# The start of a two-stage mixer kernel: the order of its first loads, and filling products on TensorE

## The chip, the cores and the metric

One core of a Trainium2 chip runs the whole program; the other cores of the chip are idle. The metric is the device time of one execution in microseconds (us), taken as the median of the runs shown.

## The reference, cut to what matters

Eight batches go through three stages: softmax attention inside chunks of 64 tokens, a mixer with a gate (moe), and a low-rank mixer with a wide channel layer (moe2).

```
attn = softmax(q_c @ k_c^T / 8); x = attn @ v_c           # 8 heads, 9 chunks of 64 tokens
h = relu(x @ w_in); u, v = halves of h (512 each)
v_n = (v - mean) / sqrt(var + 1e-6)                       # over the 512 channels
x = (u * (w_spatial @ v_n + b_spatial)) @ w_out
u = x + (x^T @ U @ V)^T;  out = u + relu(u @ w_ch1) @ w_ch2
```

## The kernel before, in words

Every large product is made of three half-precision products (`mm3`, lines 148 to 151): each operand is held as a high part and a low part, and high by high, high by low and low by high are summed. So an operand passes through ScalarE, which makes the high part, and through VectorE or GpSimd, which subtracts it from the original.

The weights arrive as 64-bit floats. To decode one tile of them, `dec_abs` (ScalarE, line 172) scales the upper words, `dec_bits` (VectorE, lines 179, 180 and 183) puts bits and sign back, and `dec_parts` makes the high part (ScalarE, line 190) and the low part (GpSimd, line 191). Eight such tiles, w_71 to w_78, are needed first: four for the half v of the first mixer (numbers 4 to 7, the tiles w_75 to w_78) and four for the half u (numbers 0 to 3, w_71 to w_74). `first_loads` (lines 423 to 459) loads them into rooms that are used later by other tiles, between the loads of the first five attention tiles; `gen_dec(0)` decodes them.

An attention tile holds two chunks of eight heads. The first nine tiles take a path of their own in single precision, `gen_first` (lines 494 to 530). For each: q is spread into a block-diagonal buffer (line 469, ScalarE, for tiles 0 to 4; by two DMAs, line 473, for 5 to 8); eight products give the scores (line 501); `a_softmax` takes maximum and difference on VectorE (384, 387) and the exponential on ScalarE (388); `a_norm` sums and divides on VectorE (393 to 396); four transpositions (514) and a copy on ScalarE (515) turn the result; eight products with v (522) give the output tile, whose high part ScalarE makes (409, or 416 for the fifth) and whose low part VectorE makes (410, 417). The values v are loaded into the tile's own `pt` space and copied on ScalarE into a block-diagonal buffer (line 484). All these buffers lie inside `wch`, the room of the later weights; tiles 5 to 8 use the places of tiles 2, 3, 4 and 2 again.

Then the first batch's mixer, `gen_moe(0)`, follows: five products with the v half of the weights (`pb<-w,xT` and `pb<-w,xd`), each evicted by ScalarE (637), normalised by VectorE and GpSimd (640 to 644, 649, 597 to 600) and scaled by VectorE (line 603, `ln_out`); eight groups with the u half (`pb<-xT,w`, evicted at line 663); the spatial product (`pb<-sp_m,vn`, with the tail of the last 64 tokens, `tl` and `vt`, in lines 679 and 680); the output product (`pb<-gt,w`); DMA transposes of it (`tr`, line 756), each one followed by a product with U (715 to 717) and V (731). The fifth `ln_out` feeds the tail: ScalarE copies it (614, 615), GpSimd makes the low part (616) and two DMAs move it (619).

The framework's scheduler decides the order of the instructions on each queue from the program's text and its priorities, so an edit in the text can move work that it doesn't name. The queue of SP issues nearly all loads, in order. Sixteen products of zeros (`NWARM`, line 450) stand at the start of TensorE's queue.

Of the kernel before, what the change touches and what calls it, by code (L numbers as in the profile page):

```python
# [8 lines left out]
F32 = mybir.dt.float32  # L9
F16 = mybir.dt.float16  # L10
# [21 lines left out]
PACE_B = 0.8  # L32
PACES = (0.0, 0.0, 1.0, 1.0, 1.0, 1.0, 0.9, 0.9)
NWARM = 16
SP_AFTER = 5
LDV = (3, 4)
MEMSET = (0, 1, 0, 1, 1)
# [63 lines left out]
def moe_kernel(  # L101
# [153 lines left out]
    def gen_dec(part):  # L255
# [17 lines left out]
        def run(names, loaded=False, step=1700.0):  # L273
            n = len(names)
            for i in range(-1, n + 2):
                if i + 1 < n and not loaded:
                    ld(names[i + 1])
                if 0 <= i < n:
                    dec_abs(names[i])
                if 0 <= i - 1 < n:  # L280
                    dec_bits(names[i - 1])
                    fin(names[i - 1])
                yield "wait", step
# [136 lines left out]

    wf = wch.rearrange("p f a k n -> p (f a k n)").bitcast(F32)

    def first_loads():

        room = []
# [22 lines left out]
        wp = ps_h.tile([128, 512], F32, tag="h", name="wp")  # L448
        for i in range(NWARM):
            nc.tensor.matmul(out=wp, lhsT=warm[:, 0:128], rhs=warm, start=True, stop=True)  # L450
        for i in range(5):
            first_qk(i)
            if i < 2:
                w()
            first_v(i)
            if i < 2:
                w()
        for i in range(4):
            w()

    def first_qk(i):
        qb, vb, kf, pt = first_bufs(i)
        if i < 5:
            qs = wf[:, 15360 + (i % 2) * 512:15360 + (i % 2 + 1) * 512]
            nc.sync.dma_start(out=qs, in_=q[i])
            nc.sync.dma_start(out=kf, in_=k[i])
            for c in range(2):
                r = slice(c * 64, (c + 1) * 64)
                nc.scalar.copy(out=qb[r, :, c, :], in_=qs[r].rearrange("p (h n) -> p h n", h=H))
            return  # L470
        for c in range(2):
            r = slice(c * 64, (c + 1) * 64)
# [2 lines left out]

    def first_v(i):
        qb, vb, kf, pt = first_bufs(i)
        vs = pt.rearrange("p a n -> p (a n)")
        if i in LDV:
            vs = sb.tile([128, 512], F32, tag="ldv", name="vs", bufs=1)  # L480
# [13 lines left out]
    def gen_first(lo, hi):  # L494

        for i in range(lo, hi):
            qb, vb, kf, pt = first_bufs(i)
            yield "wait", 2000.0
            sp = ps_acc.tile([128, H, 64], F32, tag=f"acc{i % 4}", name="sp")
            for h in range(H):  # L500
                nc.tensor.matmul(
                    out=sp[:, h, :], lhsT=qb[:, h].rearrange("p c n -> p (c n)"), rhs=kf[:, h * 64:(h + 1) * 64],
# [1 line left out]
                )  # L504
            se = kf.rearrange("p (h j) -> p h j", h=H)
            a_softmax(sp, se)
            yield "pe", 1000.0
            yield "wait", 2500.0
            a_norm(se, float(2 ** -10))
# [474 lines left out]
```

## Time and profile before

| | us |
|---|---|
| median of 3 runs (lowest, highest) | 1317.17 (1316.94, 1319.39) |
| the profiled execution, its own time | 1316.08 |
| its span, first to last instruction | 1314.3 |
| TensorE busy in the span | 1266.0 (96%) |
| VectorE, ScalarE, GpSimd busy | 529.8, 517.2, 517.3 |
| mean granted clock of TensorE, as a share of 2.4 GHz | 0.983 |

The profile is of one execution. 1.8 us of its time lie outside the span. Busy time is the time in which an engine ran at least one instruction that counts; the idle time before an instruction is put down to what ended it. PE is TensorE, PEld its weight loads, DVE VectorE, ACT ScalarE, POOL GpSimd, SP the queue that issues loads. A line number is that of the kernel's file.

### The profile page before, as it was taken

Reading aid. Unit: us, or ns where it says so; the run is one execution under the profiler, and the core shown is the slowest. Engines: PE = TensorE matmul, PEld = TensorE weight load, DVE = VectorE, ACT = ScalarE, POOL = GpSimd, SP = SyncE. Lnnn points to the kernel's source line nnn. Section 1 sums busy time; section 2 is a strip of 40 time slices with the busy share of each in tenths; the row PEclk is TensorE's granted clock in tenths of the full one; section 3 lists DMA queues with packets and bytes.
Section 4 is the critical chain, followed back from the end, with each engine's and each line's share of the span. In section 5 each row is a group of like instructions: output and inputs, shape, how many; then the busy total and the mean of one; then the engine's idle time right before and its main releaser. Section 6 shows DMA issues by size and latency. Waiting matters only on the chain.

```text
span 1314.3 us, 20540 instructions
## 1 busy us (share of the span) xinstructions
PE 1266.0 (96%) x8308; PEld 728.1 (55%) x8308; DVE 529.8 (40%) x945; ACT 517.2 (39%) x1061; POOL 517.3 (39%) x644
## 2 busy tenths in 40 slices
PE   7988888899999999999999999999999999999998
PEld 6676455445666556654665456645655565544443
DVE  8774797665343533334134514242113211221211
ACT  7765565545545433433344424323122212121110
POOL 6754887655555443534155415213111311020000
PEclk6899999899999999999999999999999999999999
DMA  8644253532223311321024101110011001000000
GB/s 285 198 143 117 88 168 100 124 103 82 61 65 77 89 33 39 77 51 42 4 65 93 49 1 33 36 41 5 0 24 34 13 0 26 20 24 1 32 0 32
DMA packets 99015, 81.43 MB, mean 62 GB/s; under 512 B 73828, under 2 KB 74468, under 8 KB 98920
## 3 DMA queue, kind: packets, MB, share of 16 engines
q1 hardware_dynamic: 97768, 75.92, 21.1%
q10 hardware_dynamic: 1152, 4.19, 0.9%
q8 instruction: 65, 1.06, 0.3%
q14 instruction: 30, 0.25, 0.1%
HBM read 53.62 MB, written 9.44 MB: 48 GB/s over the span
## 4 chain that ended last, share of the span: by engine, by line
PE 75%; DVE 8%; DMA 5%; ACT 4%; POOL 4%; issue 3%; SPq 0%; DVEq 0%; ACTq 0%; POOLq 0%
PE acc L149 8%; PE acc L151 8%; PE acc L150 8%; PE phid L151 8%; PE phid L150 8%; PE phid L149 8%; PE pb L149 7%; PE pb L150 7%; PE pb L151 7%; DVE dt L183 2%; DMA st<-in_wk_dram 2%; DVE dt L180 2%; DMA pt<-ph 1%; DMA vf<-in_v_dram 1%; DVE dt L179 1%
## 5 line engine op out<-in xcount | busy, mean ns | idle before, releaser
L815 DVE SCALAR_TENSOR_TENSOR hid<-phid,hid 128x512 f16<-128x512 f32 x144 | 99.1, 688 | 379.7 <-ACT hid L813 379.4
L150 PE MATMUL acc<-hid,wch 128*128 128x512 f16 x576 | 219.0, 380 | 0.4 <-DVE hid L815 0.4
L151 PE MATMUL acc<-hid,wch 128*128 128x512 f16 x576 | 219.1, 380 | 0.0
L149 PE MATMUL phid<-uT,wch 128*128 128x512 f16 x576 | 219.0, 380 | 0.0
L150 PE MATMUL phid<-uT,wch 128*128 128x512 f16 x576 | 218.9, 380 | 0.0
L151 PE MATMUL phid<-uT,wch 128*128 128x512 f16 x576 | 218.9, 380 | 0.0
L149 PE MATMUL acc<-hid,wch 128*128 128x512 f16 x576 | 208.5, 380 | 0.7 <-ACT hid L813 0.7
L151 PEld LDWEIGHTS <-wch 128*128 128x128 f16 x1152 | 112.9, 98 | 133.0 <-issue 2.1
L149 PEld LDWEIGHTS <-wch 128*128 128x128 f16 x1152 | 112.9, 98 | 120.7 <-issue 5.4
L150 PEld LDWEIGHTS <-wch 128*128 128x128 f16 x1152 | 113.0, 98 | 116.4 <-issue 1.6
L813 ACT ACTIVATE hid<-phid 128x512 f16<-128x512 f32 x144 | 85.5, 594 | 175.2 <-PE phid L151 174.2
L375 POOL TENSOR_TENSOR vbd<-vf,vbd 64x512 f16<-64x512 f32 x54 | 64.9, 1202 | 114.8 <-ACT vbd L374 100.9
L687 POOL TENSOR_TENSOR gt<-g,gt 128x288 f16<-128x288 f32 x64 | 50.5, 791 | 135.5 <-ACT gt L685 135.1
L753 POOL TENSOR_TENSOR tr<-x,tr 128x64 f16<-128x64 f32 x64 | 47.2, 758 | 92.0 <-issue 48.0
L362 POOL TENSOR_TENSOR qbd<-qk,qbd 64x512 f16<-64x512 f32 x54 | 64.2, 1188 | 46.5 <-ACT qbd L361 44.5
L736 POOL TENSOR_TENSOR uT<-x,uT 128x512 f16<-128x512 f32 (+7 forms) x64 | 47.5, 752 | 87.3 <-ACT uT L735 83.0
L149 PE MATMUL pb<-sp_m,vn 128*128 128x288 f16 x256 | 73.2, 286 | 6.3 <-DVE g L682 4.4
L149 PE MATMUL pb<-gt,w 128*128 128x288 f16 x256 | 73.6, 289 | 3.6 <-ACT dt L170 1.9
L150 PE MATMUL pb<-gt,w 128*128 128x288 f16 x256 | 73.8, 289 | 0.0
L151 PE MATMUL pb<-gt,w 128*128 128x288 f16 x256 | 73.8, 289 | 0.0
L150 PE MATMUL pb<-xT,w 128*128 128x288 f16 x256 | 73.7, 288 | 0.0
L151 PE MATMUL pb<-xT,w 128*128 128x288 f16 x256 | 73.7, 288 | 0.0
(175 smaller groups left out, 2340.6 us busy)
## 6 DMA issues: line engine op xcount, KB each, us to landing
st<-in_wk_dram SPq DMA_DIRECT2D x24, 512.0 KB, 3.3
out_dram<-ot SPq DMA_DIRECT2D x32, 256.0 KB, 2.1
vf<-in_v_dram SPq DMA_DIRECT2D x27, 256.0 KB, 2.6
qk<-in_q_dram SPq DMA_DIRECT2D x27, 256.0 KB, 2.7
qk<-in_k_dram SPq DMA_DIRECT2D x27, 256.0 KB, 3.0
room<-in_wk_dram SPq DMA_DIRECT2D x8, 512.0 KB, 7.0
wch<-in_wk_dram ACTq DMA_DIRECT2D x8, 512.0 KB, 3.4
wch<-in_k_dram SPq DMA_DIRECT2D x9, 256.0 KB, 4.7
```

The lines of the kernel that those rows point to most:

```text
L149: nc.tensor.matmul(out=o, lhsT=wh, rhs=xh, start=start, stop=False)
L150: nc.tensor.matmul(out=o, lhsT=wh, rhs=xl, start=False, stop=False)
L151: nc.tensor.matmul(out=o, lhsT=wl, rhs=xh, start=False, stop=stop)
L180: nc.vector.scalar_tensor_tensor(out=tb, in0=w[:, 0::2], scalar=29, in1=tb, op0=ALU.logical_shift_right, op1=ALU.bitwise_or)
L183: nc.vector.scalar_tensor_tensor(out=tb, in0=w[:, 1::2], scalar=0x80000000, in1=tb, op0=ALU.bitwise_and, op1=ALU.bitwise_or)
L362: nc.gpsimd.tensor_tensor(out=qbd[r, 1, :, c, :], in0=qv[r], in1=qbd[r, 0, :, c, :], op=ALU.subtract)
L375: nc.gpsimd.tensor_tensor(out=vbd[r, 1, :, :, c, :], in0=vf[r], in1=vbd[r, 0, :, :, c, :], op=ALU.subtract)
L687: nc.gpsimd.tensor_tensor(out=gt[:, 1, m, c], in0=g, in1=gt[:, 0, m, c], op=ALU.subtract)
L736: nc.gpsimd.tensor_tensor(out=buf[:, 1, m, c], in0=x2[:, m, t], in1=buf[:, 0, m, c], op=ALU.subtract)
L753: nc.gpsimd.tensor_tensor(out=th[:, o0:o0 + n], in0=x2[:, m, t0:t0 + n], in1=th[:, t0:t0 + n], op=ALU.subtract)
L813: nc.scalar.activation(out=hd[:, 0, :], in_=p, func=ACTF.Relu)
L815: nc.vector.scalar_tensor_tensor(out=hd[:, 1, :], in0=p, scalar=0.0, in1=hd[:, 0, :], op0=ALU.max, op1=ALU.subtract)
```

## The change

The order of the first loads: two attention tiles (q, k, v of tile 0, and q, k of tile 1) now stand ahead of the first weight, and the eight weights stand behind them in another mix. The eight decodes of `gen_dec(0)` each get a one-element copy on ScalarE that reads a new tile `turn`; `gen_first` writes one element of `turn` after the exponential of each of tiles 0 to 3, so weights 0 and 1 of the list come behind the exponential of tile 0, 2 and 3 behind that of tile 1, and so on. Ahead of the scores of tile 2 stand six products of zeros (128x512, half precision), ahead of those of tile 3 twelve, written to the bank that the scores then overwrite; their zeros are made by a memset on VectorE and one element by ScalarE after q of the tile before is copied. And v of tiles 5 to 8 is loaded by two DMAs straight into the block-diagonal buffer, without the two copies on ScalarE.

```
+FILL = {2: 6, 3: 12}
@@ gen_dec, run
-                    dec_abs(names[i])
+                    dec_abs(names[i], turn[:, i // 2:i // 2 + 1] if loaded else None)
@@ moe_kernel
+    turn = const.tile([128, 4], F32, name="turn")
@@ first_loads
-        for i in range(5):
+        for i, (n0, n1) in enumerate(((0, 0), (1, 0), (2, 1), (0, 0), (0, 4))):
             first_qk(i)
-            if i < 2:
+            for _ in range(n0):
                 w()
             first_v(i)
-            if i < 2:
+            for _ in range(n1):
                 w()
-        for i in range(4):
-            w()
+    def fill(i, wp):
+        for _ in range(FILL.get(i, 0)):
+            nc.tensor.matmul(
+                out=wp.rearrange("p h j -> p (h j)"), lhsT=idle[i][:, 0:128], rhs=idle[i], start=True, stop=True)
+    idle = {}
@@ first_qk, i < 5
+            if i + 1 in FILL:
+                z = idle[i + 1] = sb.tile([128, 512], F16, tag=("ph", "kd", "se")[i], name="idle", bufs=1 + (i == 2))
+                nc.vector.memset(z, 0.0)
+                nc.scalar.activation(out=z[0:1, 0:1], in_=qs[0:1, 0:1], func=ACTF.Copy, scale=0.0)
@@ first_v
+        if i >= 5:
+            for c in range(2):
+                r = slice(c * 64, (c + 1) * 64)
+                nc.sync.dma_start(out=vb[r, :, :, c, :], in_=v[i][r].rearrange("p (a c e) -> p a c e", a=4, c=2))
+            return
@@ gen_first
             sp = ps_acc.tile([128, H, 64], F32, tag=f"acc{i % 4}", name="sp")
+            fill(i, sp)
@@ gen_first, after a_softmax
+            if i < 4:
+                nc.scalar.copy(out=turn[0:1, i:i + 1], in_=se[0:1, 0, 0:1])
```

In the changed file the lines stand one to 22 further down than before (172 is 173, 388 is 389, 469 is 478, 484 is 503, 603 is 625, 679 is 701).

The order on ScalarE from the first copy of q on, before. `room` is a weight as loaded, `dt` a weight half decoded, `wch` the attention buffers.

```order
L469 COPY wch<-wch 64x8x64 x2
L172 ACTIVATE dt<-room 128x512
L484 COPY wch<-wch 64x8x64 x2
L172 ACTIVATE dt<-room 128x512
L190 CAST w_75<-dt 128x512
L469 COPY wch<-wch 64x8x64 x2
L190 CAST w_76<-dt 128x512
L172 ACTIVATE dt<-room 128x512
L484 COPY wch<-wch 64x8x64 x2
L388 ACTIVATE wch<-wch 128x512
```

The same place now:

```order
L478 COPY wch<-wch 64x8x64 x2
L503 COPY wch<-wch 64x8x64 x2
L478 COPY wch<-wch 64x8x64 x2
L483 ACTIVATE idle<-wch 1x1
L503 COPY wch<-wch 64x8x64 x2
L478 COPY wch<-wch 64x8x64 x2
L483 ACTIVATE idle<-wch 1x1
L389 ACTIVATE wch<-wch 128x512
L528 COPY turn<-wch 1x1
L171 COPY dt<-turn 1x1 x2
L173 ACTIVATE dt<-room 128x512 x2
```

The exponential of tile 0 stood behind three weight steps and now stands ahead of all of them, behind the copies of v of tile 1 and q of tile 2.

The order on VectorE up to the fifth `ln_out`, before (the rows from the fourth `ln_out` on; `rz` is the normalised tile).

```order
L603 TENSOR_SCALAR rz<-rz,mv,y 128x512
L640 BN_STATS bs<-rz 128x6
L180 SCALAR_TENSOR_TENSOR dt<-st,dt 128x512
L393 TENSOR_REDUCE sm<-wch 128x8
L212 TENSOR_TENSOR v_88<-dt,v_88 32x288
L642 BN_AGGR mv<-bs 128x2
L183 SCALAR_TENSOR_TENSOR dt<-st,dt 128x512
L394 TENSOR_SCALAR sm<-sm 128x8
L644 TENSOR_SCALAR mv<-mv 128x1
L395 RECIPROCAL sm<-sm 128x8
L396 TENSOR_TENSOR wch<-wch,sm 128x512
L179 TENSOR_SCALAR dt<-dt 128x512
```

The same place now:

```order
L625 TENSOR_SCALAR rz<-rz,mv,y 128x512
L181 SCALAR_TENSOR_TENSOR dt<-st,dt 128x288
L180 TENSOR_SCALAR dt<-dt 128x512
L184 SCALAR_TENSOR_TENSOR dt<-st,dt 128x288
L181 SCALAR_TENSOR_TENSOR dt<-st,dt 128x512
L411 TENSOR_TENSOR xT<-of,xT 128x4x128
L184 SCALAR_TENSOR_TENSOR dt<-st,dt 128x512
L213 TENSOR_TENSOR v_88<-dt,v_88 32x288
L662 BN_STATS bs<-rz 128x6
L664 BN_AGGR mv<-bs 128x2
L666 TENSOR_SCALAR mv<-mv 128x1
```

Ahead of the fifth `ln_out`, eight softmaxes and four low parts (410) stood in VectorE's queue; now nine and seven do. GpSimd's queue holds the same instructions ahead of its part of the tail (616) as before.

The order on TensorE at the last of the first tail products, before (L501 are scores, L522 values, L514 transpositions of an attention tile):

```order
L679 LDWEIGHTS tl
L679 MATMUL pb<-sp_t_84,tl 128x288
L680 LDWEIGHTS vt_89
L680 MATMUL pb<-sp_t_85,vt_89 128x288
L501 MATMUL sp<-wch 128x64
L522 MATMUL of<-wch 128x64 x8
L514 MATMUL tp<-ident,wch 128x128 x2
L149 LDWEIGHTS vn
```

The same place now:

```order
L701 LDWEIGHTS tl
L701 MATMUL pb<-sp_t_84,tl 128x288
L702 LDWEIGHTS vt_89
L702 MATMUL pb<-sp_t_85,vt_89 128x288
L150 LDWEIGHTS vn
L150 MATMUL pb<-sp_m,vn 128x288
```

The values of one attention tile, with a part of its scores and transpositions, stood between the tail products and the next spatial product, and now stand ahead of the tail.

## Rows read from the trace of the kernel before

**Rows 1.** Windows: us, busy PE, PEld, DVE, ACT, POOL (instructions), clock, DMA, GB/s.
```profile
0.00:7.75 7.75, 6.55 (x31) 3.62 (x32) 3.02 (x6) 3.38 (x5) 6.81 (x10) 1.00 0.73 236
...
31.40:36.00 4.60, 4.60 (x22) 4.31 (x21) 1.08 (x3) 4.53 (x9) 4.60 (x5) 0.50 0.65 185
...
41.90:46.00 4.10, 4.10 (x26) 2.41 (x25) 0.46 (x2) 4.00 (x8) 3.95 (x4) 1.00 0.57 174
46.00:87.10 41.10, 35.64 (x253) 26.71 (x252) 39.66 (x82) 27.99 (x60) 24.58 (x37) 0.96 0.53 173
...
290.00:1314.30 1024.30, 1017.89 (x6573) 561.57 (x6571) 321.20 (x591) 337.12 (x686) 324.99 (x444) 1.00 0.15 37
```

**Rows 2.** Windows of the first 12 us, of the half clock, up to 87.1.
```profile
0.00:4.00 4.00, 2.80 (x7) 1.01 (x8) 2.65 (x4) 1.86 (x3) 3.47 (x8) 1.00 0.50 165
4.00:8.00 4.00, 4.00 (x26) 2.78 (x24) 0.62 (x3) 1.74 (x4) 3.34 (x3) 1.00 0.97 316
8.00:12.00 4.00, 0.54 (x4) 0.51 (x3) 3.72 (x6) 3.37 (x6) 1.57 (x1) 0.89 1.04 412
11.10:38.40 27.30, 23.60 (x104) 21.89 (x104) 23.61 (x49) 23.41 (x41) 18.77 (x16) 0.50 0.83 275
0.00:87.10 87.10, 73.70 (x436) 57.62 (x437) 73.22 (x148) 64.71 (x122) 55.88 (x66) 0.82 0.66 219
```

**Rows 3.** Chain of waits, 82 to 93 us: start, duration, engine and output.
```profile
87.10 0.56 DVE rz L603
```

**Rows 4.** Timeline of VectorE, 36 to 62 us: start, duration, line, operation.
```profile
38.50 0.67 DVE L410 TENSOR_TENSOR xT<-of,xT 128x512 f16<-128x512 f32 x1
39.10 0.68 DVE L183 SCALAR_TENSOR_TENSOR dt<-room,dt 128x512 uint32<-128x512 uint32 x1
39.70 0.16 DVE L394 TENSOR_SCALAR sm<-sm 128x8 f32<-128x8 f32 x1
...
58.33 0.68 DVE L183 SCALAR_TENSOR_TENSOR dt<-st,dt 128x512 uint32<-128x512 uint32 x1
...
61.44 1.46 DVE L183 SCALAR_TENSOR_TENSOR dt<-st,dt 128x512 uint32<-128x512 uint32 x1
```

**Rows 5.** Timeline of GpSimd, the same stretch.
```profile
61.19 1.16 POOL L191 TENSOR_TENSOR w<-dt,w 128x512 f16<-128x512 f32 x1
```

**Rows 6.** Timeline of TensorE, 0 to 130 us.
```profile
1.20 5.13 PE L450 MATMUL wp<-warm 128*128 128x512 f16 x16 [1.20 <-DVE warm L440]
6.17 1.89 PE L501 MATMUL sp<-wch 128*128 128x64 f32 x16
...
17.23 3.68 PE L501 MATMUL sp<-wch 128*128 128x64 f32 x16 [2.06 <-ACT wch L469]
...
92.08 0.29 PE L679 MATMUL pb<-sp_t,tl 128*128 128x288 f16 x1
...
92.98 1.95 PE L522 MATMUL of<-wch 128*128 128x64 f32 x16
...
103.57 0.29 PE L149 MATMUL pb<-gt,w 128*128 128x288 f16 x1
...
104.89 0.56 PE L501 MATMUL sp<-wch 128*128 128x64 f32 x4
...
115.57 0.23 PE L715 MATMUL pb<-tr,u_h 128*128 128x128 f16 x1 [3.17 <-DMA tr<-tr]
...
127.65 0.23 PE L715 MATMUL pb<-tr,u_h 128*128 128x128 f16 x1 [1.02 <-DMA tr<-tr]
```

**Rows 7.** Timeline of ScalarE, 0 to 20 us.
```profile
3.62 1.24 ACT L469 COPY wch<-wch 64x512 f32<-64x512 f32 x2 [1.41 <-DMA wch<-in_q_dram]
...
7.05 0.67 ACT L172 ACTIVATE dt<-room 128x512 f32<-128x512 f32 x1 [2.18 <-DMA room<-in_wk_dram]
...
14.86 0.63 ACT L388 ACTIVATE wch<-wch 128x512 f32<-128x512 f32 x1
```

**Rows 8.** The one-element copies of line 170 on ScalarE.
```profile
L170 ACT COPY dt<-rz x5: 173/190/191, 76.0 to 157.6; 1x1 f32<-1x1 f32 x5
```

## The prediction

> **What bounds the kernel now.** I read the windows first, because the busy shares of the whole span mix stages with different limits. From 290 us on TensorE is busy for 1017.89 of 1024.30 us [rows 1]: only work taken from TensorE could gain anything there, and the change takes none. In the first 87.1 us TensorE is busy for only 73.70 us [rows 2], and 27.3 of them, from 11.1 to 38.4, run at a granted clock of 0.50, the 1.2 GHz level. So whatever this change is worth is settled near the start. Work that TensorE does before some fixed point is shifted as a whole if that point shifts. From the first product of the last group of transposes on (127.65 us, [rows 6]) the instructions of every engine stand in the same order in both kernels. What counts is therefore when that point is reached; the rest follows at the same distance.
>
> Next, the chain of waits from there back. It comes from TensorE's tail products to the fifth `ln_out` on VectorE, which starts at 87.10 [rows 3]. Is it VectorE that sets this start? From 46 to 87.1 VectorE is busy for 39.66 of 41.10 us [rows 1]: it has no slack, while TensorE idles there for 5.5. Its idle time lies ahead: 4.73 us at the start, 3.52 from 31.4 to 36, 3.64 from 41.9 to 46 [rows 1], 1.44 after that. Up to 87.1 it is busy for 73.22 us, so 13.88 are idle [rows 2]; 0.55 are left over for the rest. The way to the tail is then VectorE's work plus its idle time, and I count the change in these two.
>
> **The change, part by part.**
>
> *Idle time of VectorE.* The first score ends at 6.17 + 1.89 = 8.06 [rows 6], and VectorE can then begin the first softmax, instead of a weight at 7.75. Two memsets of zeros come before that; they can cost no more than two steps of 0.60; I take 0.5 for both, between nothing and 1.2. So 4.5 us stay idle early (4.73 before, the start 0.3 us later, the memsets inside). Maximum and difference take two steps of 0.60 (start to start, as from 38.50 to 39.10, [rows 4]), to 9.3. Then VectorE has nothing until the first exponential, since the weights wait for it. That exponential now stands behind the copies of v of tile 1 and q of tile 2. v of tile 1 is the seventh load on the queue, at 2.1 MB in all. By 4 us 0.66 MB are moved, by 8 us 1.92 [rows 2], and the rest goes at 412 GB/s: 8.4 us. The first weight gives the lag from moved to usable: with q and k ahead of it (0.26 MB each, the weight 0.52) its end is at 1.05 MB, reached near 5.2, and ScalarE uses it at 7.05 [rows 7]: 1.8. So the copies begin at 10.2, take 2 x 1.24 [rows 7] to 12.7, and the exponential, 0.63 [rows 7], ends near 13.5 (before: 14.86 + 0.63 = 15.5). VectorE idles for 4.2 there. The two later stretches close, because the work that the exponentials released is now in front of them; I keep 0.5. Sum 9.2 for 13.88: **-4.7**.
>
> *VectorE's work ahead of the tail.* By the order, one softmax and three low parts more stand ahead of the fifth `ln_out`. A softmax has four wide steps of 0.60 and two small ones of some 0.2 [rows 4]: 2.8. The low parts are 3 x 0.60 = 1.8. With the memsets: **+5.1**. The scheduler took these forward since in its account attention is further on; they are not gained, only moved, and appear again below.
>
> *Beside GpSimd.* An instruction of VectorE that reads two operands in SBUF sometimes takes 1.46 us instead of 0.68, and then GpSimd runs one of its own beside it [rows 4, 5]: 0.78 for each meeting. Sixteen such lengthenings stand in VectorE's timeline before 87.1. In the two idle stretches that close, GpSimd has nine instructions, eight of them wide [rows 1], and these met nobody. Work that moves there meets them. The bounds are 0 and 8 x 0.78 = 6.2. Between them I take three: later on two in three of GpSimd's wide subtractions met something, and of VectorE's steps that move in about half (maximum, sum, reciprocal) read one operand. **+2.3**.
>
> For this the Trainium skill, SBUF — State Buffer, § Who interferes with whom, has a rule: the pair of ports that VectorE shares with GpSimd is an exclusive lock, an instruction with two inputs in SBUF competes for it with any GpSimd instruction that reads SBUF, and the loser blocks fully. The size agrees, 0.78 of a 1.16 us instruction; taken at its word for all eight it would put the sum at the second rival's instead of mine.
>
> The tail would so start 2.7 us later than before, near 89.8.
>
> *After the tail.* What VectorE did earlier TensorE did earlier too. By the order the values of one tile, 1.95 us at 92.98 [rows 6], and one of its eight scores, 0.24, no longer stand between the tail products and the output product at 103.57; 0.56 us of scores leave its first blocks at 104.89 [rows 6]; and some work leaves the transposes, whose waits for DMAs of 3.17 and 1.02 us [rows 6] take part of that back (some 0.4 is left). **-3.2**. Bounds: 1.5 if those waits grow by what leaves, 4.5 if all of it counts and 1.3 us of waits go too.
>
> *The products of zeros.* Sixteen of them take 5.13 us [rows 6], so six take 1.9 and twelve 3.8. They stand in gaps of TensorE before the third and fourth scores, which wait for copies on ScalarE (2.06 us at 17.23, [rows 6]). They cost nothing as long as q arrives no sooner; without that cover at most the overlap of a group of 1.9. What they are for is the clock: a group of scores took 1.89 at the full one and 3.68 at half [rows 6]. From 11.1 to 38.4 TensorE has only 11.8 us of full-clock work. As VectorE bounds this stretch, holding the clock counts for the early scores alone, and these are in the idle times above.
>
> *ScalarE.* The one-element copies take 0.19 each [rows 8], fourteen of them 2.7 us; eight copies of v, of the size of q's (1.24 for two, [rows 7]), go. Both are at ScalarE's margins: after 46 us it is busy for 27.99 of 41.10 [rows 1]. Nothing. The direct loads of v are four more instructions on SP's queue, which runs at 0.53 of the DMA time there [rows 1]. Nothing, below or above by a few tenths.
>
> Sum: -4.7 + 5.1 + 2.3 - 3.2 = -0.5. Against the profiled execution's own 1316.08 this is 1315.6. The median of the runs is 1317.17, 1.1 above that execution, so the forecast is **1316.7, no change**. A measurement of this kernel can tell 0.2%, 2.6 us.
>
> **The rivals.**
>
> *The front carries.* The added 2.3 do not come, and since everything on VectorE falls elsewhere beside GpSimd, five of the sixteen old meetings go as well: -3.9. Then -4.7 + 5.1 - 3.2 - 3.9 = -6.7, **1310.5**. For it: a meeting is decided by tenths of a us, and all of VectorE's instructions move; and TensorE at the full clock has its tiles ready earlier. Against it: VectorE is still full for 41 us, and I see nothing that spreads the two engines apart.
>
> *GpSimd's lock.* All eight instructions in the closed stretches block VectorE: +6.2 instead of 2.3, so +3.4, **1320.6**. It decides where VectorE works from 31.4 to 46, and is slower than 0.2% from seven meetings of the eight on (the other terms give -2.8, so 5.4 us are needed, 5.4 / 0.78 = 6.9). For it: both engines are full in one stretch. Against it: of the instructions that move there many read one operand. This is the case that the rule in the SBUF page of the Trainium skill, § Who interferes with whom, makes.
>
> *The zeros do not hold the clock.* The change would not do what it says: the third and fourth scores still run at 0.50, and one group more of 3.68 instead of 1.89 falls on the chain: at most +1.8, **1318.5**. For it: TensorE is idle around the groups of zeros too. Against it: the sixteen products at the start were followed by a group at full speed [rows 6].
>
> **How the numbers follow.** Forecast 0.47, the front carries 0.25, the lock 0.18, the clock 0.10. The forecast's own spread is that of its terms: about 3 us either way (the lengthenings by 2.3, what follows the tail by 1.5), so some 0.07 of it is faster by over 0.2%, and 0.03 slower; of the clock's case 0.02 is slower. Faster: 0.25 + 0.08 = 0.33. Slower: 0.17 + 0.03 + 0.02 = 0.22. The same: 0.45. The range goes from 1310.0, just beyond the front's case, to 1321.0, just beyond the lock's; half of each case lies outside by the size of its own terms, 2 in 10 in all.
>
> **What would show it.** In the profile after: the first score's maximum on VectorE at 8, the first exponential near 13; a clock of 1.00 from 12 to 38; VectorE without idle stretches over 1 us after 14; the fifth `ln_out` near 90 and the first output product near 103. The forecast is wrong if that `ln_out` stands before 86 (the front carries) or after 93 (the lock, then with VectorE instructions of 1.4 us and more beside GpSimd between 25 and 46). A clock of 0.50 anywhere from 14 to 30 speaks for the third rival. If the fifth `ln_out` is at 90 and the time is off nevertheless, the step after the tail was wrong.

## The result, and the profile after

| | before | after |
|---|---|---|
| median (lowest, highest), us | 1317.41 (1316.94, 1319.39) | 1327.28 (1327.06, 1332.01) |
| ratio after to before, 95% interval | | 1.0086 (1.0070, 1.0103) |
| profiled execution, its span, us | 1316.08, 1314.3 | 1332.01, 1330.2 |

The changed kernel is slower: the medians are 9.9 us apart, 0.75%, and the recorded ratio says 0.86%, some 11 us. The forecast was 1316.7, no change, and its range ended at 1321.0; a slower kernel had a chance of 0.22. The profiled execution of the changed kernel took 4.7 us more than its own median, so lengths read in its trace may be a few us larger than those between the medians. What an experiment costs or gains is therefore read from its recorded ratio to the kernel before, which was run again beside each group of experiments; its trace, of one execution, only tells where.

The windows of VectorE's way to the tail, and of the two stretches behind it, changed kernel (columns as in [rows 1]):

```profile
0.00:96.89 96.89, 87.76 (x544) 65.79 (x545) 84.99 (x158) 67.09 (x140) 57.99 (x66) 0.86 0.67 211
...
46.00:100.00 54.00, 46.80 (x324) 36.69 (x322) 51.73 (x93) 33.96 (x73) 37.13 (x47) 0.87 0.56 172
100.00:150.00 50.00, 37.54 (x253) 25.19 (x254) 21.59 (x36) 20.42 (x50) 25.54 (x30) 0.86 0.30 79
```

And the same two stretches of the kernel before:

```profile
46.00:100.00 54.00, 47.10 (x350) 36.65 (x349) 45.13 (x92) 37.19 (x79) 32.10 (x46) 0.97 0.49 158
100.00:150.00 50.00, 42.24 (x290) 28.43 (x288) 26.96 (x51) 25.80 (x62) 29.38 (x37) 0.93 0.42 108
```

The fifth `ln_out` starts at 96.89 instead of 87.10 [rows 3]. Up to it VectorE is busy for 84.99 us instead of 73.22 and idle for 11.9 instead of 13.88 [rows 2]. TensorE's mean granted clock from 46 to 150 us is 0.87 and 0.86, against 0.97 and 0.93: in the changed kernel some 27 us of this stretch are at the half clock, in the kernel before some 10.

Where does VectorE's extra time come from? Its timeline in the changed kernel (start, duration, engine, line, operation, output and input, count, and in brackets the idle time before and what ended it):

```profile
9.34 0.69 DVE L385 TENSOR_REDUCE mx<-sp 128x8 f32<-128x512 f32 x1 [4.43 <-PE sp L521]
...
12.77 0.69 DVE L394 TENSOR_REDUCE sm<-wch 128x8 f32<-128x512 f32 x1 [2.01 <-ACT wch L389]
...
37.26 0.13 DVE L218 COPY vbd<-w 1x1 f16<-1x1 f16 x1
...
42.07 3.33 DVE L395 TENSOR_SCALAR sm<-sm 128x8 f32<-128x8 f32 x1
42.14 3.53 DVE L180 TENSOR_SCALAR dt<-dt 128x512 uint32<-128x512 uint32 x1
```

and GpSimd's:

```profile
20.60 2.72 POOL L192 TENSOR_TENSOR w<-dt,w 128x512 f16<-128x512 f32 x2 [13.21 <-ACT w L191]
...
37.15 0.95 POOL L895 MEMSET vt<- 128x1024 f16 x1 [0.74 <-DVE sp_t L218]
38.06 1.79 POOL L232 TENSOR_TENSOR sp_m<-st,sp_m 128x576 f16<-128x576 f32 x1
39.80 1.05 POOL L898 MEMSET sp_t<- 128x1152 f16 x1
...
41.83 1.80 POOL L904 MEMSET qbd<- 128x2048 f16 x1
43.58 1.80 POOL L904 MEMSET vbd<- 128x2048 f16 x1
45.34 1.33 POOL L192 TENSOR_TENSOR w<-dt,w 128x512 f16<-128x512 f32 x1
```

The same of the kernel before, GpSimd and then VectorE:

```profile
10.36 1.57 POOL L191 TENSOR_TENSOR w<-dt,w 128x512 f16<-128x512 f32 x1 [2.97 <-ACT w L190]
...
24.37 0.95 POOL L873 MEMSET vt<- 128x1024 f16 x1 [1.74 <-DVE sp_t L217]
...
27.58 2.07 POOL L882 MEMSET qbd<- 128x2048 f16 x1
29.60 1.82 POOL L882 MEMSET vbd<- 128x2048 f16 x1
31.39 1.15 POOL L191 TENSOR_TENSOR w<-dt,w 128x512 f16<-128x512 f32 x1
```

```profile
27.84 1.85 DVE L394 TENSOR_SCALAR sm<-sm 128x8 f32<-128x8 f32 x1
27.90 1.78 DVE L410 TENSOR_TENSOR xT<-of,xT 128x512 f16<-128x512 f32 x1
```

The idle time before the first exponential is much as foretold. But GpSimd now does nothing for 13.21 us, until the first weight comes at 20.60 (before: 10.36). Behind the fourth weight stand six memsets; with a subtraction for another tile (`sp_m`, 1.79 us) among them they take GpSimd from 37.15 to 45.4, 8.2 us. They write `vt`, `sp_t`, `u_l`, `u_h`, `qbd` and `vbd` and have nothing to do with the weight; a one-element copy on VectorE (line 218, `after`) holds each of them until the fourth weight is decoded. Before they ran from 24.37 to 31.4. Two things follow. The low part of the fifth weight, which stands behind them, is ready at 46.7 instead of 32.5. And a step of VectorE that took 0.4 us elsewhere takes 3.53 beside the two long memsets: it ends only when both are over. A small step just ahead of it (line 395, 0.15 us elsewhere) is held as long, 3.33 us, so this trace doesn't tell which of the two the memsets hold.

At the tail, TensorE in the changed kernel:

```profile
105.95 0.40 PE L701 MATMUL pb<-sp_t,tl 128*128 128x288 f16 x1 [8.17 <-DMA tl<-vn]
...
127.79 0.29 PE L737 MATMUL pb<-tr,u_h 128*128 128x128 f16 x1 [4.45 <-DMA tr<-tr]
```

and the queue of SP:

```profile
89.83 12.42 SPq L160 DMA_DIRECT2D st<-in_wk_dram  x4
102.31 1.16 SPq L641 DMA_DIRECT2D tl<-vn  x2
```

and the queue of SP in the kernel before:

```profile
89.80 1.73 SPq L619 DMA_DIRECT2D tl<-vn  x2
```

The first tail product starts 13.9 us later than before (92.08, [rows 6]), 4.1 more than the fifth `ln_out`, after a wait of 8.17 us, and then lasts 0.40 instead of 0.29: the granted clock is 0.50 from 102.4 to 109.2. The two DMAs of the tail (line 641) stand on SP's queue behind four loads of weights, the last of which is out at 102.3. The first product with U is 12.2 us later (115.57, [rows 6]), the end of this execution 15.9.

### The profile page after: what moved, and what is told of

Same layout as the page of the kernel before. It is cut to its first block, busy times and chain, and to the rows that moved or that the text cites. A ratio compares the mean times of both kernels' runs of the same rounds, so it can differ in the third digit from the quotient of the medians.

```text
span 1330.2 us, 20590 instructions
## 1 busy us (share of the span) xinstructions
PE 1275.1 (96%) x8326; PEld 728.2 (55%) x8326; DVE 541.0 (41%) x947; ACT 513.1 (39%) x1067; POOL 520.5 (39%) x644
## 3 DMA queue, kind: packets, MB, share of 16 engines
q8 instruction: 65, 1.06, 0.3%
## 4 chain that ended last, share of the span: by engine, by line
PE 72%; DVE 9%; DMA 7%; ACT 5%; POOL 3%; issue 3%; SPq 0%; DVEq 0%; ACTq 0%; POOLq 0%
PE acc L150 8%; PE acc L152 8%; PE acc L151 8%; PE phid L151 8%; PE phid L150 8%; PE phid L152 8%; PE pb L150 7%; PE pb L151 7%; PE pb L152 7%; DVE dt L184 2%; DVE dt L181 2%; DMA pt<-ph 2%; DMA vf<-in_v_dram 2%; DMA st<-in_wk_dram 1%; DMA room<-in_wk_dram 1%
## 5 line engine op out<-in xcount | busy, mean ns | idle before, releaser
L775 POOL TENSOR_TENSOR tr<-x,tr 128x64 f16<-128x64 f32 x64 | 47.9, 769 | 92.2 <-issue 46.7
L363 POOL TENSOR_TENSOR qbd<-qk,qbd 64x512 f16<-64x512 f32 x54 | 64.3, 1191 | 47.4 <-ACT qbd L362 45.4
```

The costliest lines, as they stand in the source:

```text
L363: nc.gpsimd.tensor_tensor(out=qbd[r, 1, :, c, :], in0=qv[r], in1=qbd[r, 0, :, c, :], op=ALU.subtract)
L775: nc.gpsimd.tensor_tensor(out=th[:, o0:o0 + n], in0=x2[:, m, t0:t0 + n], in1=th[:, t0:t0 + n], op=ALU.subtract)
```

## The experiments

Ratios are to the kernel before, with the 95% interval; the changed kernel stands at 1.0086.

| run | what | ratio (interval) | fifth `ln_out`, us |
|---|---|---|---|
| e1_no_turn | change without the weights' wait | 1.0009 (0.9995, 1.0022) | 89.4 |
| e2_no_fill | change without zeros | 1.0059 (1.0042, 1.0075) | 89.9 |
| e3_memsets_free | change, memsets not held | 1.0011 (1.0001, 1.0020) | 86.1 |
| e4_v_copied | change, v copied as before | 1.0098 (1.0083, 1.0114) | 100.5 |
| e5_memsets_dve | change, two memsets on VectorE | 1.0037 (1.0023, 1.0051) | 89.4 |
| e6_before_free | before, memsets not held | 1.0026 (1.0005, 1.0047) | 82.9 |
| e7_no_turn_free | e1 and e3 | 1.0013 (1.0002, 1.0025) | 83.4 |
| e8_free_no_fill | e2 and e3 | 1.0003 (0.9990, 1.0016) | 82.8 |
| e9_gate_last | change, two memsets later still | 1.0098 (1.0073, 1.0123) | 95.0 |
| e10_before_v_direct | before, v direct | 1.0041 (1.0022, 1.0061) | 88.4 |
| e11_no_turn_no_fill | e1 and e2 | 1.0007 (0.9992, 1.0022) | 86.3 |
| e12_before_late | before, memsets later | 1.0070 (1.0047, 1.0093) | 87.9 |
| e13_tail_queue | change, tail's DMAs on another queue | 1.0083 (1.0066, 1.0100) | 95.9 |
| e14_v_direct_held | e10 with zeros ahead of the tail | 1.0025 (1.0010, 1.0039) | 88.8 |
| e15_tail_queue_held | e13 with zeros ahead of the tail | 1.0072 (1.0057, 1.0087) | 95.5 |
| e16_free_tail_queue | e3 and e13 | 0.9997 (0.9984, 1.0009) | 85.6 |

Each edit lets the scheduler order the work anew, so a run tells of its edit with all that the scheduler then moves.

### Which part of the change

**e1_no_turn**

```
-                    dec_abs(names[i], turn[:, i // 2:i // 2 + 1] if loaded else None)
+                    dec_abs(names[i], None)
...
-            if i < 4:
-                nc.scalar.copy(out=turn[0:1, i:i + 1], in_=se[0:1, 0, 0:1])
```

> The changed kernel without the one-element copies of turn, so that the eight weights no longer wait for exponentials; loads, products of zeros and direct loads of v stay. Theory A (the weights wait, GpSimd stands idle from 7 to 20 us, and VectorE and GpSimd then do the same work side by side and late): at least half of the 10 us come back, 1322 or less, and GpSimd's first subtraction of a weight moves from 20.6 us to 14 or earlier. Theory B (the work that the order takes ahead of the fifth ln_out is the cost; 9 softmaxes and 9 low parts stand ahead of it here too): 1325 to 1329.

1.0009: the loss is gone, as theory A had it. GpSimd's first subtraction moved to 13.16. But theory B is not tested: the expectation counts nine softmaxes and nine low parts ahead of the fifth `ln_out`, and in the trace it is eight and five (line 411), against nine and seven in the changed kernel. The ninth maximum comes behind it:

```profile
35.06 3.54 DVE L180 TENSOR_SCALAR dt<-dt 128x512 uint32<-128x512 uint32 x1
...
89.42 0.55 DVE L623 TENSOR_SCALAR rz<-rz,mv,y 128x512 f32<-128x512 f32 x1
...
100.59 0.69 DVE L385 TENSOR_REDUCE mx<-sp 128x8 f32<-128x512 f32 x1 [1.62 <-PE sp L521]
```

So a part of the work that theory B blames has gone along with the waiting. A VectorE step of 3.54 us beside the long memsets (35.06) is in this trace as well, but the memsets come 7 us earlier and VectorE has 14.2 us idle ahead of its fifth `ln_out`: the stall alone is not the price. That it costs only where VectorE is full fits this, and is not shown.

**e2_no_fill**

```
-FILL = {2: 6, 3: 12}
+FILL = {}
```

> The changed kernel without the products of zeros, their memsets and one-element writes. Theories A and B: they lie in gaps of TensorE and VectorE bounds the stretch, so within 2.6 us of the changed kernel, 1325 to 1330, with the scores of the third and fourth tile at half the clock. Rival (the zeros hold TensorE or VectorE up): 1324 or less. Rival (the held clock is worth something): 1330 or more.

1.0059, 1324.7: between the two answers. Without zeros TensorE is at the half clock from 11.7 to 39.0, as before, and the kernel is some 3.5 us faster, though the two intervals overlap at their ends. The zeros do hold the clock until 23.9, and this is worth nothing here. In this trace the memsets start 4 us earlier (32.98), so the gain need not be the zeros' own time: e8, below.

**e4_v_copied**

```
-        if i >= 5:
-            for c in range(2):
-                r = slice(c * 64, (c + 1) * 64)
-                nc.sync.dma_start(out=vb[r, :, :, c, :], in_=v[i][r].rearrange("p (a c e) -> p a c e", a=4, c=2))
-            return
```

> The changed kernel with v of tiles 5 to 8 loaded whole and copied by ScalarE as before. Theories A and B: ScalarE has 4.9 us more in all and is not the bound, within 2.6 us of the changed kernel, 1325 to 1330. Rival (the direct loads in pieces of 64 values are slow and hold later loads up): 1324 or less.

1.0098, the same as the changed kernel within the intervals. The direct loads are no part of its loss.

### The memsets

**e3_memsets_free**: the copies of `after` that hold the memsets are left out.

```
-    after(7, vt2[:, 0, :])
...
-    for t in (sp_t2[:, 0, :], u_l[:, 0, :], u_h[:, 0, :]):
-        after(7, t)
...
-        after(7, u)
```

The number is that of a weight; they are decoded in the order 4, 5, 6, 7, 0, 1, 2, 3, so 7 is the fourth of them.

> The changed kernel without the one-element copies on VectorE that keep six memsets of GpSimd (8.2 us at 37.2 to 45.4) behind the fourth weight; they then stand ahead of the first weight's low part, in GpSimd's idle time from 7 to 20 us. Theory A with the memsets as its main price: VectorE loses the 3.5 us instruction beside the two long memsets, the fifth weight's low part moves from 46.7 to under 40 us, the fifth ln_out from 96.9 to 92 or earlier, 1319 to 1322. Theory A with the waiting alone: the fifth ln_out moves by under 2 us, 1325 to 1328.

1.0011: all but 1.3 us of the loss is gone. GpSimd and the window of VectorE's way to the tail (0 to the fifth `ln_out`) in this run:

```profile
7.32 0.95 POOL L894 MEMSET vt<- 128x1024 f16 x1
...
12.00 1.80 POOL L900 MEMSET vbd<- 128x2048 f16 x1
```

```profile
0.00:86.14 86.14, 75.68 (x479) 56.91 (x480) 77.17 (x142) 61.94 (x128) 54.64 (x64) 0.88 0.67 213
```

The memsets lie in GpSimd's idle time. VectorE is busy for 77.17 us and idle for 9.0, and the fifth `ln_out` comes at 86.14, 10.8 us earlier than in the changed kernel; the fifth weight's low part is ready at 39.1. It is a little more than either case of the expectation gave. So e1 and e3 each undo the loss: of the edits, it needs both, the weights that wait and the memsets that wait for a weight.

How does the `ln_out` come 10.8 us earlier? By the two windows 2.9 us are idle time, and VectorE has 16 instructions fewer ahead of it (142 for 158): six one-element copies, six steps of weights, three low parts and the last step of the ninth softmax. The scheduler put the last ten behind the `ln_out`. Steps that are longer than usual account for some 2 us (estimate: each one's excess over the usual duration of its kind, overlapping ones once), so some 6 are work that was moved. Such an excess stands in e3 too, some 4.5 us over the kernel before, and e3 is only 0.1% slower than that.

This leaves a rival. In the changed kernel, e4, e9, e13 and e15, nine softmaxes and six or seven low parts (line 411) stand ahead of the fifth `ln_out`, and 0.7 to 1.0% is lost; in all other runs no more than eight whole softmaxes, mostly with four or five low parts, and of them e2 loses 0.6 and e12 0.7, the others 0.4 or less. No run has the changed kernel's order on VectorE without late memsets, so what the order costs by itself is open.

**e5_memsets_dve**

```
         after(7, u)
-        nc.gpsimd.memset(t, 0.0)
+        nc.vector.memset(t, 0.0)
```

> The changed kernel with the two long memsets (qbd and vbd, 3.6 us of GpSimd) given to VectorE, still behind the fourth weight. It tells what the memsets cost through VectorE's stall beside them (an instruction of 3.5 us for 0.4) from what they cost by standing in GpSimd's queue ahead of the fifth weight's low part. Either way both go here, and VectorE pays for the two memsets itself, an estimate of 1.2 to 1.8 us each from its memset of 128x2048 in 1.76. Theory M (it is the two long ones, by stall and queue): 1320 to 1323. Rival (it is the place of the whole block, late weights after all): 1325 or more.

1.0037, 1321.5: in the range of theory M. Over half of the loss goes when VectorE does the two long memsets, although it pays for them itself (less than estimated); two low parts and the end of the ninth softmax are behind the fifth `ln_out` here as well:

```profile
37.68 0.91 DVE L904 MEMSET qbd<- 128x1024 uint32 x1 [0.16 <-DVE sm L396]
38.76 0.91 DVE L904 MEMSET vbd<- 128x1024 uint32 x1 [0.16 <-DVE qbd L904]
```

**e9_gate_last**: the two long memsets behind the eighth weight (number 3) instead of the fourth.

```
-        after(7, u)
+        after(3, u)
```

> The changed kernel with only the two long memsets (qbd, vbd) put behind the eighth weight instead of the fourth: they are still GpSimd's and still run beside a full VectorE, but stand behind all eight low parts in the queue. If they cost by their place in the queue (the low parts of the fifth to eighth weight wait for them): those come some 3.5 us earlier, 1319 to 1323, as with the memsets on VectorE. If they cost by the stall of VectorE beside them: the stall goes along to a place near 60 us, 1325 or more.

1.0098: the loss stays, though the fifth to eighth weights' low parts are ready 4 to 9 us earlier (42.4 to 54.9 instead of 46.7 to 63.6). The stall goes along with the memsets; VectorE and GpSimd of this run:

```profile
58.19 1.43 DVE L381 COPY xT<-xd 128x256 f16<-128x256 f16 x2
59.53 2.10 DVE L625 TENSOR_SCALAR rz<-rz,mv,y 128x512 f32<-128x512 f32 x1
```

```profile
57.66 1.80 POOL L904 MEMSET qbd<- 128x2048 f16 x1 [1.11 <-DVE vbd L218]
59.41 1.95 POOL L904 MEMSET vbd<- 128x2048 f16 x1
```

In the changed kernel such pairs of copies (line 381) took 0.61 and 0.35 us, and `ln_out` 0.53 to 0.55 four times of five. So the place of the two long memsets ahead of the low parts is not what costs by itself; that they run beside a VectorE that has no time to lose fits both runs.

**e12_before_late**: in the kernel before, all six memsets behind the seventh weight (number 2).

```
-    after(7, vt2[:, 0, :])
+    after(2, vt2[:, 0, :])
...
-        after(7, u)
+        after(2, u)
```

> The kernel before with the six memsets behind the seventh weight instead of the fourth, which puts them some 8 us later, ahead of the eighth weight's low part alone, into the stretch from 31 to 46 where VectorE has 7 us to spare. If late memsets cost by themselves: 1321 or more. If they cost only where low parts wait behind them and VectorE is full: 1315 to 1319.

1.0070, 1325.4: late memsets alone cost 8 us in a kernel without any other part of the change. VectorE has the same instructions ahead of its fifth `ln_out` as before, so here it is not moved work. But the way is another than in the changed kernel: the fifth `ln_out` is only 0.8 us later (87.85). TensorE at the tail:

```profile
93.38 0.40 PE L679 MATMUL pb<-sp_t,tl 128*128 128x288 f16 x1 [2.76 <-DMA tl<-vn]
```

TensorE waits for 2.76 us, its clock is 0.50 from 92.0 to 102.3, and the first output product comes at 109.15 instead of 103.57 [rows 6]: 5.6 us out of 0.8.

**e6_before_free**, **e7_no_turn_free** and **e8_free_no_fill** combine edits that are shown above; each is that of e3 on another kernel.

> The kernel before with the six memsets freed from the fourth weight; they stand at the head of GpSimd's queue. Theory M (they cost where VectorE is busy and weights wait behind them): there they stood from 24.4 to 31.4 and VectorE lost about 2.2 us beside them, but now the first weight's low part, at 10.36 us, waits until some 15.5, so the early products come later: between -3 and +3, 1314 to 1320. Rival (GpSimd's queue is what bounds the start): 1312 or less.

1.0026, 1322.0: slower, and beyond what was expected (1320 at most; by the ratio +3.4 us where +3 was the limit). The fifth `ln_out` comes 4.2 us earlier than before, but the first output product at 104.36, 0.8 later, and the end is no earlier: a gain on VectorE's way to the tail is not kept behind it.

> The changed kernel without the copies of turn and with the memsets freed. Theory M (the memsets are the whole price and they are late only because of turn): turn gone gives what the memsets gave, so the two do not add up: within 2.6 us of either alone, 1315 to 1320. Rival (the waiting of the weights has a price of its own beside the memsets): 1314 or less.

1.0013, 1320.1: at the upper end of what was expected; the two don't add up.

> The changed kernel with the memsets freed and without the products of zeros. If the zeros hold the clock and this is worth something once the memsets are out of the way: 1320 or more. If they only change the order of the work, as the 3 us of the run without them suggests: 1314 to 1318.

1.0003, against 1.0011 with the zeros: once the memsets are out of the way the zeros cost nothing and give nothing that can be measured. So the 3.5 us of e2 are hardly the zeros' own time; they came with another order, in which the memsets are earlier and eight softmaxes stand ahead of the fifth `ln_out`.

**e11_no_turn_no_fill** (the edits of e1 and e2)

> The new order of the loads and the direct v, without turn and without zeros. If the run without turn still carries the price of the zeros (3 us in the run without them): 1312 to 1316, faster than both kernels. If the zeros cost nothing by themselves and only moved the memsets (they stood 4 us earlier there): 1316 to 1320.

1.0007, the second case. The new order of the loads, with v direct, is worth nothing that can be measured.

### What happens behind the tail

**e10_before_v_direct**: in the kernel before, the five lines that e4 takes out, and nothing else.

> The kernel before with the direct loads of v for tiles 5 to 8 and nothing else. With the run that took them out of the changed kernel they should be worth nothing or little: 1315 to 1319. Rival (they are a part of the loss, or a gain that the rest hides): outside of that.

1.0041: the rival. Of the whole change this part alone, which costs nothing in the changed kernel, makes the kernel before 5.4 us slower. The scheduler's order on VectorE changes along with it; the fifth `ln_out` is 1.3 us later. **e14_v_direct_held** tests why that became 5:

```
...
                 for st in range(4):
                     mm3(o, vn[:, st, d], vn[:, 4 + st, d], sp_m[:, 0, st, c], sp_m[:, 1, st, c], st == 0, False)
+                if b == 0 and m == 1 and hf == 0:
+                    for _ in range(12):
+                        nc.tensor.matmul(out=o[:, 0:192], lhsT=vn[:, 0, d], rhs=zero, start=False, stop=False)
```

> The kernel before with the direct loads of v, which was 5 us slower though its fifth ln_out came only 1.3 us later, and with twelve products of zeros ahead of the spatial product that precedes the first tail products. They fill about 1 of the 1.97 us for which TensorE waited there, after which its granted clock was 0.50 from 93.0 to 103.3. Theory K (a somewhat longer wait makes the clock fall, and this is most of the 5 us): no half clock near 93 to 103, 1316 to 1319. Rival (the 5 us are the changed order on VectorE and ScalarE): 1321 or more.

Windows of e10 and of e14 from 93 us on, and the first tail product of e14:

```profile
93.00:103.00 10.00, 9.84 (x44) 7.84 (x45) 4.28 (x10) 2.26 (x6) 2.98 (x4) 0.50 0.29 86
```

```profile
93.00:103.00 10.00, 9.52 (x81) 8.24 (x82) 6.17 (x14) 4.16 (x11) 5.13 (x6) 1.00 0.30 86
```

```profile
93.48 0.28 PE L690 MATMUL pb<-sp_t,tl 128*128 128x288 f16 x1 [2.00 <-DMA tl<-vn]
```

In e14 the tail product still waits, 2.00 us, as in e10 (1.97), but the clock stays at 1.00, TensorE does 81 products in these 10 us instead of 44, and the first output product comes at 105.64 instead of 109.53. So between these two executions, in which the fifth `ln_out` is 0.3 us apart, the half clock there costs some 4 us. The ratios say less: 1.0025 against 1.0041 is 2 us, with intervals that overlap, between the two cases of the expectation. That the length of the wait decides is not borne out, since it is the same in both. The zeros are not all that differs: ten products of scores that e10 has just ahead of the wait come behind the tail in e14.

**e13_tail_queue**, the tail's DMAs on ScalarE's queue:

```
-                nc.sync.dma_start(out=tl[g, j, :], in_=vn[h, 8, :])
+                (nc.scalar if b == 0 else nc.sync).dma_start(out=tl[g, j, :], in_=vn[h, 8, :])
```

> The changed kernel with the two DMAs of the first tail issued from ScalarE's queue instead of SP's, where they stood behind four loads of weights that waited for VectorE's weight steps. Everything else stands in the same order. Theory Q (part of the loss after the fifth ln_out is this queue): the DMAs start when GpSimd's halves end (99.7 and 101.3 instead of 102.3 and 102.9), the first tail product comes 2 us earlier, 1323 to 1326. Rival (the tail is late by VectorE and GpSimd alone): within 1 us of the changed kernel.

```profile
104.00 0.40 PE L701 MATMUL pb<-sp_t,tl 128*128 128x288 f16 x1 [7.74 <-DMA tl<-vn]
```

The first tail product is 2 us earlier in the trace, half of it because `ln_out` is, but 1.0083 is the ratio of the changed kernel within the interval. Taking the DMAs off SP's queue gets nothing back that can be measured: the first of them is issued at 100.04 instead of 102.31, but from there to the product it takes 4.0 us instead of 3.6. **e15_tail_queue_held** adds 46 products of zeros in the way of e14, and **e16_free_tail_queue** joins e3 and e13.

> The changed kernel with the tail's DMAs on ScalarE's queue and 46 products of zeros ahead of the spatial product that precedes the first tail products, some 4 to 5 us of TensorE's wait of 8.17. Theory K: TensorE is at the full clock from there to 120 us, some 3 us faster than with the queue alone. Rival: as with the queue alone, within 1 us, or slower by what the zeros overrun.

1.0072, its median 1.8 us under e13's, with intervals that overlap. The half clock at the tail shrinks from 98.2 to 108.5 in e13 to 104.9 to 108.3. The direction is that of theory K, the size about half.

> The changed kernel with the memsets freed (0.1% over the kernel before) and the tail's DMAs on ScalarE's queue. There the second of them was issued at 92.5, 2.7 us after GpSimd's half. Theory Q: the output product, 106.8 there, comes some 3 us earlier, 1313 to 1316, faster than both kernels. Rival: 1317 to 1319.

0.9997: the time of the kernel before, between the two cases. The first output product comes at 105.21 for 106.78 in e3, half of what theory Q asked. No version here beats the kernel before.

## Why the prediction was wrong

The forecast was -0.5 us, added up to the products behind the tail; in the profiled executions the first product with U is 12.2 us later. Its terms, forecast and read: idle time of VectorE -4.7 and -2.0, work ahead of the tail +5.1 and +5.1, steps beside GpSimd +2.3 and +6.7, behind the fifth `ln_out` -3.2 and +2.4.

*The early idle time: right.* 8.7 us were to be idle until the first exponential is out; in the trace it is 7.8, namely 1.4 at the start, 4.43 before the maximum (which came at 9.34, since the sixteen products at the start took 6.37 and not 5.13 us) and 2.01 before the first sum. The exponential ended at 12.7, foretold 13.5.

*The later idle time: wrong by 3.6 us in the changed kernel.* "I keep 0.5": it is 4.1 us, in pieces of 1.06 and less; in e3, without the late memsets, only 0.3 is in one piece, and the whole idle time is 9.0 where 9.2 was forecast.

*The work ahead of the tail: right.* VectorE is busy 11.8 us longer. Of these some 6.7 are lengthenings (11.2 us before, 17.9 after, each the excess over the usual duration of its kind, overlapping ones once; the difference is 6 to 7 by how much of an excess is counted); 5.1 are left, as forecast, and the instructions that came to stand ahead of the fifth `ln_out` are the ones it names.

*Beside GpSimd: this is the first step that failed.* It said 2.3, within 0 and 6.2; it is 6.7. The step looked at the eight instructions of GpSimd that stood in the idle stretches of the kernel before, and took their places as given. GpSimd's queue holds the same instructions ahead of its part of the tail, but at other times: six memsets hang on the fourth weight, the fourth weight now hangs on the exponentials, and so they move from 24.4 to 37.2 and into VectorE's busy stretch. A wait was added by the change, and what was queued behind the waiting instruction was not followed. Of the 6.7 the memsets make directly some 1.6: VectorE loses some 3.4 us beside the two long ones, and lost some 1.8 beside the memsets before (27.84, 27.90). The others are meetings with the rest of GpSimd's queue. The rival of GpSimd's lock was right on the size, 6.2, and its sign came, a fifth `ln_out` after 93 and steps of 1.4 us and more between 25 and 46; it was wrong on what does it, and its 1320.6 is still 6.7 us short.

*What the lock is here.* In the trace the step of 3.53 us waits beside instructions that read nothing. The rule of the Trainium skill that the prediction drew on (SBUF — State Buffer, § Who interferes with whom) speaks in the place cited of instructions with two inputs beside a GpSimd that reads; the same section says that `tensor_scalar` and copies in their two-port modes compete with GpSimd as well, and that whoever comes first keeps the pair for the whole instruction. The trace agrees with that second rule, with 3.53 us for 0.42, and 1.43 and 2.10 in e9; whether these steps run in such a mode no row shows. That it is this lock is argued from the places and durations; no run separates it from another cause.

*After the tail: the second step that failed, by what it left out.* It said -3.2, within -1.5 and -4.5. From the fifth `ln_out` to the first product with U it was 28.5 us before and is 30.9: +2.4. Three windows divide this stretch (columns as in [rows 1]): to the first tail product, to the first output product and to the first product with U; before, then after:

```profile
87.10:92.08 4.98, 3.54 (x32) 3.15 (x31) 1.19 (x3) 4.54 (x10) 3.46 (x3) 1.00 0.37 118
92.08:103.57 11.49, 11.49 (x98) 9.63 (x98) 7.32 (x14) 6.27 (x14) 6.01 (x7) 1.00 0.25 76
103.57:115.57 12.00, 8.83 (x76) 7.44 (x73) 4.78 (x10) 6.76 (x17) 6.29 (x8) 1.00 0.48 136
```

```profile
96.89:105.95 9.06, 0.89 (x9) 0.68 (x8) 5.60 (x5) 3.72 (x7) 5.08 (x4) 0.80 0.40 130
105.95:116.83 10.88, 10.88 (x77) 8.15 (x78) 5.25 (x10) 3.94 (x9) 4.72 (x6) 0.85 0.01 2
116.83:127.79 10.96, 6.20 (x50) 4.59 (x48) 3.71 (x4) 4.72 (x14) 6.10 (x8) 0.93 0.29 75
```

What the step did price came true. TensorE had less to do: a clock of 0.85 in the second window is 3.3 us at half speed, so at the full one it would take 9.2 (estimate), 2.2 less than before, and the third window is 1.0 shorter; that is the forecast's 3.2, the third window in part by luck, since TensorE does 2.6 us less there and waits longer. The step put two things at nothing without a reason. The way from the fifth `ln_out` to the first tail product grew by 4.1 us: the first of the tail's two DMAs is issued 5.4 us behind the `ln_out` instead of 2.7, held on SP's queue by the four loads, and from its issue to the product it is 3.6 us instead of 2.3. And behind its wait of 8.17 us, where it waited for nothing before, TensorE runs at the half clock: the other 1.6. The clock was watched only where the change meant to hold it. Why the transfer takes longer is open, and e13 shows that the queue alone is not what the kernel loses by.

*"The rest follows at the same distance": right as far as it can be told.* The first product with U is 12.2 us later, the sixth and the ninth `ln_out`, at 148.2 and 175.1 us, 11.9 each. In this execution the shift then grows in small steps to 15.9 at the end, but it took 4.7 us more than the median, and the medians are only 9.9 apart. And in e6 and e8 a fifth `ln_out` that is 4 us early gains nothing at the end.

*The products of zeros* were rightly costed at nothing by themselves (e8). The forecast "a clock of 1.00 from 12 to 38" was wrong: it holds to 23.9, where TensorE has just waited for 2.53 us, and is 0.50 from there to 37.5. The sign named for the third rival, a half clock between 14 and 30, so came, but not what that rival says: the third and fourth scores took 1.89 and 2.00 us, at the full clock.

```profile
12.22 1.89 PE L521 MATMUL sp<-wch 128*128 128x64 f32 x16
...
17.43 2.00 PE L521 MATMUL sp<-wch 128*128 128x64 f32 x16
...
24.01 1.09 PE L536 MATMUL tp<-ident,wch 128*128 128x128 f32 x4 [2.53 <-DVE wch L397]
```

*The direct loads of v: right in the changed kernel (e4), wrong as a rule (e10)*: "Nothing, below or above by a few tenths" was 5.4 us in the other surroundings.

One reading in it is off, and nothing rests on it: the 27.3 us from 11.1 to 38.4 are the length of the stretch at the half clock, and TensorE is busy for 23.60 of them [rows 2].

What stays open is how the 9.9 us divide among stall, moved work, later low parts and clock. In e1 and e3 several of them go together, and the two runs that were made for the clock (e14, e15) move the median by about 2 us, inside their intervals.

## What to carry to other kernels

When an edit makes a step later, list everything that is held by that step, also what is held for order's sake alone, and ask beside what it will run in its new place: here it was six memsets that needed nothing, and without their gate the same change costs 0.1% instead of 0.9. What else the scheduler moves with such an edit has to be read from the trace before the gain is put down to the one thing that was edited. A gate that was placed for one order of the work must be placed again when the order changes. And a few us at a point where TensorE has to wait are priced by the clock it gets afterwards as well as by the wait: in e12's trace 0.8 us became 5.6.

## What the runs showed of the hardware

- Two memsets of 1.80 us on GpSimd, one behind the other, kept a `TENSOR_SCALAR` of VectorE that usually takes 0.42 us for 3.54 us in e1 (35.06): through both, not until the end of the first. In the changed kernel one took 3.53 beside the same pair, with a smaller one ahead of it that took 3.33.
- The memset of the same buffer took 1.80 us on GpSimd (128x2048 of 16 bits) and 0.91 on VectorE (e5), where it ran as 128x1024 of 32 bits.
- A wait of 2.00 us ahead of the tail was followed by the full clock in e14, one of 1.97 by the half clock in e10 for 10 us, in one execution each. Ahead of the wait e14 had twelve products of zeros behind the spatial products, and not the ten scores that e10 had there.
- From the issue of the tail's first DMA to the first tail product it was 2.3 us in the kernel before, 3.6 in the changed kernel and 4.0 in e13, where another queue issued it.
